# Linear attention and a bilinear feed-forward on one core: inputs of units 4 to 6 loaded later, two weight pieces in their place, and a new order of tiles

## The chip, the cores and the metric

The kernel runs on one core of a Trainium2 chip. The metric is device time in microseconds (us) of that core for one launch. A core has five engines with a queue each: TensorE (PE, matmuls), VectorE (DVE), ScalarE (ACT), GpSimd (POOL) and SyncE (SP), which here only issues DMAs.

## What is computed

A gated linear attention, followed by a feed-forward layer with a product in the middle. All in float32, with `q`, `k`, `v`, `f_logit` of shape (4, 8, 768, 48):

```python
f = 1.0 / (1.0 + np.exp(-f_logit))
for t in range(S):                      # S = 768, per batch and head
    state = f[t][:, None] * state + outer(k[t], v[t])
    y[t] = q[t] @ state
x = y.transpose(0, 2, 1, 3).reshape(B * S, H * D)   # (3072, 384)
out = ((x @ w_a) * (x @ w_b)) @ w_out               # 384 -> 1536 -> 384
```

The weights come in a 64-bit format and have to be turned into float32 on the core before they can be used.

## The kernel before

**Attention** is cut into 16 units. A unit is four heads of one batch over half of the sequence (384 tokens). The two units of a half make a block of 384 tokens: units 0 and 1 block 0, units 2 and 3 block 1, and so on. Each unit's inputs f, k, q and v lie in one of three sets of tiles (`sets[u % 3]`), and `load_unit(u, names)` puts their loads in SP's queue: two DMAs each for f, k and q and one for v. A unit goes through these steps: `front` (ACT: sigmoids; POOL: an affine step; DVE: scans and the scaling of k and q), `scores` (PE) and `mask` (DVE), `turn` (PE transposes k into PSUM) and `turned` (ACT copies it out), `within` (PE: the part of y inside a chunk), `gains` (PE: the growth of the state) and `carried` (DVE sums the states), `across` (PE: the part of y from the states), `out_of_bank` (copies y out of PSUM) and `stored` (DMAs that put it into `xT`, the transposed input of the feed-forward). `y_of(u)` is the last two together. A unit uses two PSUM tiles, `ps_x` and `ps_y`, in turn with its neighbours: `turn(3)` writes the tile from which unit 2's y is copied.

**Weights** come in 20 pieces, called `todo` and counted here from 0: pieces 0 to 13 are columns of `w_b` and `w_a` in turn, 14 to 19 rows of `w_out`. Pieces 0 and 1 hold tile 0 of 128 columns, 2 and 3 tiles 1 and 2, 4 and 5 tiles 3 and 4, 6 and 7 tiles 5 and 6, 8 and 9 tiles 7 and 8, 10 and 11 tiles 9 and 10, 12 and 13 tile 11. `load_weights(n)` issues the next n loads; apart from pieces 4 and 5, they go to four places in turn (`raw`), so the load of piece i waits until the piece that lies in its place has been read. `begin(n)` puts the conversion's first two steps of the pieces below n into the queues: four ACT operations (L58, L59, L62, L63) and one on POOL (L60). `end(n)` adds the rest on DVE (L68, L73, three parts, one for each third of the rows) and, for most pieces, the load of one more piece. `begin(7.5)` stands for a piece's first step alone. `convert(n)` is `end` up to n with the next `begin`.

**Feed-forward up** in this stage is done by tiles: `up(blk, ft)` computes tile ft of both products for block blk, with three matmuls for b and then three for a, into two of four PSUM banks (`ps_f`). `product()` takes the oldest tile not yet multiplied: ACT copies b to `x_sums` (L615) and DVE multiplies a by it into `groups` (L617). After that the two banks are free.

**Order.** All of it stands in `by_quotients` within a manual schedule: each engine executes its instructions in the order in which the program gives them, with semaphores between engines. From the start to unit 3's y the order is written out by hand. Then the loop over `ups` does 14 tiles of blocks 0 and 1, in each round with `convert(needed(i))`, `up`, `end(7 + n)`, `product()` and `begin(ended[0] + 2)`. What follows (the rest of the tiles, units 4 to 15, `down`, and from block 2 on a scheme of products with fewer multiplications) is ordered by a planner that works with assumed durations; it does not use the loading of units 4 to 6.

In the kernel before, `stored(u)` itself loads unit u + 3 for u of 2 and 3, so the inputs of unit 5 stand in SP's queue right behind unit 2's y, and those of unit 6 right behind unit 3's. Unit 4's f is loaded early (at `scores(2)`), its k, q and v after unit 6's inputs.

Of the kernel before, what the change touches and what calls it, by code (L numbers as in the profile page):

```python
# [136 lines left out]
def by_quotients(ctx, tc, q, k, f_logit, v, moe_w_a, moe_w_b, moe_w_out, out, ident, weights, bad):  # L137
# [4 lines left out]
    NKT, NFT, DM = w_ba.shape[2], w_out.shape[1], out.shape[1]  # L142
    NH = S // BLK
    NQ = H // 4
# [6 lines left out]
    NSET = 3  # L151
# [47 lines left out]
    def load_unit(u, names="fkqv"):  # L199
        for do in loads_of(u, names):  # L200
            do()
# [37 lines left out]
    def load_weights(n=1):  # L239
        for _ in range(n):  # L240
            if len(raws) == len(todo):
                return
            dst, src, (k, m) = todo[len(raws)]
            raw = dst
            if src.dtype != FP32:

                if len(raws) in EARLY:
                    raw = groups[:, EARLY.index(len(raws))].bitcast(mybir.dt.uint64)
                else:
                    raw = next(raw_places)  # L250
                raw = raw[:, 0:k * m].rearrange("p (k m) -> p k m", k=k)
            nc.sync.dma_start(out=raw, in_=src)
            raws.append(raw)

    def begin(n):

        while 2 * n > begun[0] < 2 * len(todo):
            i, second = divmod(begun[0], 2)
            dst, src, shape = todo[i]
            if not second:  # L260
                going.append(
                    from_double(
                        nc, dst, raws[i], shape[0], next(blocks), bits[i % len(bits)], sign, whole, shape[0] == NKT
                    )
                    if src.dtype != FP32 else iter(())
                )
            next(going[i], None)
            begun[0] += 1

    def end(n):  # L270

        while ended[0] < min(n, len(todo)):
            begin(ended[0] + 1)
            next(going[ended[0]], None)
            ended[0] += 1
            if ended[0] > 2 and ended[0] - 1 not in EARLY:
                load_weights()
# [15 lines left out]
    def halves(x):  # L293
        return x.rearrange("p n s -> p (n s)")
# [59 lines left out]
    def tokens(n, c, p):  # L354

        return slice(n * BLK + c * C + p * SUB, n * BLK + c * C + p * SUB + SUB)

    def each():
        for n in range(2):
            for c in range(NC):  # L360
                yield n, c, (n * NC + c) * SUB
# [5 lines left out]
    def home(u):  # L367

        return ps_y if u in (1, 3) else ps_x
# [5 lines left out]
    def pair_of(x):  # L375

        return [x[:, i] for i in range(2)]

    def scores(u):
        t = sets[u % NSET]  # L380
        qf, kf = halves(t["q"]), halves(t["k"])
        ps = pair_of(home(u))
        for n, c, o in each():
            for h in range(2):
                for p in range(2):
                    r = slice(R * h, R * h + D)
                    nc.tensor.matmul(  # L387
                        ps[h][SUB * p:SUB * p + SUB, o:o + SUB],
                        lhsT=kf[r, tokens(n, c, p)],
                        rhs=qf[r, tokens(n, c, p)],  # L390
                        start=True,
                        stop=True,
                    )

    def mask(u):

        at = sb1.tile([128, 2, BLK], FP32, tag="at", name="at")
        to, x = (y.rearrange("s h (o t) -> s h o t", t=SUB) for y in (at, home(u)[:, :, 0:BLK]))
        tri = causal.unsqueeze(1).unsqueeze(1)
        nc.vector.tensor_tensor(to, x, tri.broadcast_to((128, 2, 2 * NC, SUB)), ALU.mult)  # L400
        live[u]["at"] = at

    def turn(u):

        kf = halves(sets[u % NSET]["k"])
        live.setdefault(u, {})["kT"] = sb1.tile([128, 2, NC, 128], FP32, tag="kT", name="kT")
        ps = live[u]["turned"] = [ps_f[idle.pop(0)] for _ in range(2)] if u in FIRST else pair_of(away(u))
        for n in range(2):
            for c in range(NC):
                o = n * BLK + c * C  # L410
                nc.tensor.transpose(ps[n][:, c * C:c * C + C], kf[:, o:o + C], ident)  # L411
# [10 lines left out]
    def gains(u, chunks=range(NC)):  # L422

        _, half, _ = unit(u)
        t, kT = sets[u % NSET], live[u]["kT"]
        last = half == NH - 1
        ps = live[u]["turned"]
        for n in range(2):
            for c in chunks:
                for p in range(2):  # L430
                    if last and c == NC - 1 and p == 1:
                        continue
                    for h in range(2):
                        r = slice(SUB * p, SUB * p + SUB)
                        nc.tensor.matmul(  # L435
                            ps[p][R * h:R * h + D, (n * NC + c) * D:(n * NC + c) * D + D],
                            lhsT=kT[r, n, c, R * h:R * h + D],
                            rhs=t["v"][r, n, c, h * D:h * D + D],
                            start=True,
                            stop=True,  # L440
                        )
        if chunks[0]:
            return
        st = sb3.tile([128, NJ, 2, D], FP32, tag="st", name="st")
        before = live[u - NQ]["st"][NJ] if half else None
        live[u]["st"] = [before] + [st[:, j] for j in range(NJ - 1 if last else NJ)]

    def carried(u, js=range(NJ)):

        for j in js:  # L450
            if j + 1 < len(live[u]["st"]):
                carry(u, j)
        if js[-1] == NJ - 1:
            give_back(live[u]["turned"])
# [38 lines left out]
    def across(u):  # L493

        b, half, qd = unit(u)
        qf, st, ps = halves(sets[u % NSET]["q"]), live[u]["st"], live[u]["y"]

        order = [(n, c, o, p) for n, c, o in each() for p in range(2)]
        if u in FIRST:

            order = sorted(order[::-1], key=lambda x: -x[3])
        elif half:
            order = [(n, c, o, p) for n, c, o in reversed(list(each())) for p in range(2)]
        for n, c, o, p in order:
            j = 2 * c + p
            if j == half == 0:
                continue
            for h in range(2):
                r, e = slice(R * h, R * h + D), R * (p ^ h)
                nc.tensor.matmul(  # L510
                    ps[p][e:e + D, o:o + SUB],
                    lhsT=st[j][r, n],
                    rhs=qf[r, tokens(n, c, p)],
                    start=False,
                    stop=True,
                    skip_group_check=True,
                )
# [13 lines left out]
    def stored(u):  # L531

        for do in stores_of(u):
            do()
        if u >= NQ:
            load_unit(u + NSET)

    def stores_of(u):

# [43 lines left out]
    def up(blk, ft):  # L583

        for _, _, _, do, *args in up_steps(blk, ft):
            do(*args)
# [22 lines left out]
    def product():  # L609

        if not factors:
            return
        blk, ft, ps = factors.pop(0)
        b_sb = next(b_copies)
        nc.scalar.copy(b_sb, ps["b"][:, 0:BLK])  # L615
        a, b = (x.rearrange("p (g t) -> p g t", g=NTG) for x in (ps["a"][:, 0:BLK], b_sb))
        nc.vector.tensor_tensor(products(blk)[:, :, ft], a, b, ALU.mult)  # L617
        give_back(ps.values())
# [321 lines left out]
    with tc.manual_schedule():  # L940
# [9 lines left out]
        fronts = {u: front(u) for u in (0, 1, 3)}  # L950
# [95 lines left out]
        product()  # L1046
        carried(2)
        begin(6)
        next(fronts[3])
        up(0, 2)  # L1050
        across(2)
        end(6)
        y_of(2)
        load_weights(2)
        turn(3)
        turned(3)
        scores(3)
        product()
        begin(7)
        up(0, 3)  # L1060
        mask(3)
        begin(7.5)
        within(3)
        gains(3)
        product()
        carried(3)
        begin(8)
        up(0, 4)
        end(8)
        begin(9)  # L1070
        across(3)
        y_of(3)
        load_unit(4, "k")
        load_unit(4, "q")
        load_unit(4, "v")
        product()


        ups = [(0, 5), (1, 0)]
        for i in range(6, NFT):  # L1080
            ups += [(1, i - 5), (0, i)]
        ups += [(1, i) for i in range(NFT - 5, NFT)]
        alone = len(todo) - 6
        for n, (blk, i) in enumerate(ups[0:alone]):
            convert(needed(i))
            up(blk, i)
            end(7 + n)
            product()
            begin(ended[0] + 2)


        w_out_sums, (w_before, w_over) = list(combine_w_out()), combine_w_ba()
# [520 lines left out]
```

## Time and profile before

| what | value |
|---|---|
| median of 3 runs | 606.46 us (605.02 to 607.68) |
| the profiled execution | 607.98 us, its span 606.3 us |
| mean granted PE clock | 0.983 |
| PE busy | 571.5 us, 94% of the span |
| PE weight load busy | 511.3 us, 84% |
| DVE busy | 411.3 us, 68% |
| ACT busy | 268.6 us, 44% |
| POOL busy | 77.2 us, 13% |
| chain that ended last | PE 84%, DVE 8%, DMA 3%, issue 2%, ACT 2% |

The span runs from the first to the last instruction of the core; the device time is somewhat longer. Busy shares are means over the whole span. The chain is followed back from the last instruction, at each step to what released it. In rows of the timeline the columns are start, length, engine, line, operation, tile written and tiles read, count, and in brackets the idle time just before with what ended it. A tile in `up` shows as 12 matmuls[...].

### The profile page before, as it was taken

How to read it: one execution, taken by the hardware profiler on the slowest of the kernel's cores; microseconds unless marked ns; L12 is line 12 of the kernel's file. 1: busy time of each engine (PE TensorE's matmuls, PEld its weight loads, DVE VectorE, ACT ScalarE, POOL GpSimd, SP SyncE). 2: the span in 40 equal slices, each digit the busy share in tenths (PEclk: the TensorE clock that was granted, in tenths of full speed). 3: DMA queues.
4: the chain of work that ended last, by engine and by line, in shares of the span. 5: the costliest groups of instructions: out<-in, count | busy, mean ns of one | idle time of the engine just before them, and what ended most of it. 6: DMA issues, size and time to landing. Idle time of an engine off the chain costs nothing.

```text
span 606.3 us, 13891 instructions
## 1 busy us (share of the span) xinstructions
PE 571.5 (94%) x5778; PEld 511.3 (84%) x5778; DVE 411.3 (68%) x788; ACT 268.6 (44%) x505; POOL 77.2 (13%) x71
## 2 busy tenths in 40 slices
PE   1588799999999999999999999999999999999995
PEld 1555355556899999999989999999999999999995
DVE  6996344579969769967895768746775165745741
ACT  6488658962232455336532353326331335134300
POOL 6344234534200000000000000000000000000000
PEclk9988989999999999999999999999999999999998
DMA  9695796149843143035002420023001100000000
GB/s 208 188 282 160 255 230 206 52 73 172 160 126 105 50 96 79 3 91 133 3 1 78 113 61 2 1 69 77 2 2 47 47 0 1 2 27 0 1 28 32
DMA packets 33272, 49.42 MB, mean 82 GB/s; under 512 B 3952, under 2 KB 24976, under 8 KB 33200
## 3 DMA queue, kind: packets, MB, share of 16 engines
q1 hardware_dynamic: 30000, 42.38, 25.5%
q0 software_dynamic: 3056, 5.92, 5.7%
q8 instruction: 47, 0.77, 0.6%
q14 instruction: 25, 0.20, 0.1%
q10 hardware_dynamic: 144, 0.15, 0.1%
HBM read 33.23 MB, written 4.72 MB: 63 GB/s over the span
## 4 chain that ended last, share of the span: by engine, by line
PE 84%; DVE 8%; DMA 3%; issue 2%; ACT 2%; SPq 1%; DVEq 0%; ACTq 0%
PE ps_f L717 35%; PE ps_f L810 27%; PE ps_f L595 14%; PE ps_y L484 2%; PE ps_x L387 2%; DVE sums L709 1%; PE ps_y L510 1%; DVE inv L329 1%; PE ps_x L411 1%; PE ps_x L435 1%; DMA raw<-in_moe_w_b_dram 1%; DMA xT<-y 1%; DVE groups L709 1%; DVE q_in L333 1%; DVE groups L316 1%
## 5 line engine op out<-in xcount | busy, mean ns | idle before, releaser
L595 PE MATMUL ps_f<-xT,w_ba 128*128 128x384 f32 x288 | 102.2, 513 | 8.0 <-DMA xT<-y 5.7
L595 PEld LDWEIGHTS ps_f<-xT,w_ba 128*128 128x128 f32 x288 | 56.4, 200 | 49.0 <-issue 12.7
L1261 ACT COPY sums<-ps_f 128x384 f32<-128x384 f32 x120 | 57.5, 480 | 75.8 <-PE ps_f L717 68.1
L1261 ACT COPY groups<-ps_f 128x384 f32<-128x384 f32 x120 | 57.8, 481 | 62.8 <-PE ps_f L717 39.9
L717 PE MATMUL ps_f<-xT,w_ba 128*128 128x192 f32 x384 | 78.4, 327 | 0.0
L717 PEld LDWEIGHTS ps_f<-xT,w_ba 128*128 128x128 f32 x384 | 64.8, 190 | 0.2
L717 PE MATMUL ps_f<-groups,w_ba 128*128 128x192 f32 x288 | 55.4, 327 | 0.0
L717 PE MATMUL ps_f<-x_sums,raw 128*128 128x192 f32 x288 | 54.0, 331 | 1.2 <-DVE groups L709 0.9
L810 PE MATMUL ps_f<-w_out,sums 128*128 128x192 f32 x288 | 52.2, 329 | 0.0
L810 PE MATMUL ps_f<-w_out,groups 128*128 128x192 f32 x288 | 51.7, 328 | 0.0
L717 PEld LDWEIGHTS ps_f<-x_sums,raw 128*128 128x128 f32 x288 | 46.9, 190 | 4.3 <-DVE groups L709 1.8
L810 PE MATMUL ps_f<-spare,sums 128*128 128x192 f32 x288 | 49.0, 326 | 0.0
L717 PEld LDWEIGHTS ps_f<-groups,w_ba 128*128 128x128 f32 x288 | 47.9, 190 | 0.5 <-ACT groups L1261 0.3
L810 PEld LDWEIGHTS ps_f<-w_out,sums 128*128 128x128 f32 x288 | 47.1, 190 | 1.0 <-DVE o L845 0.5
L810 PEld LDWEIGHTS ps_f<-w_out,groups 128*128 128x128 f32 x288 | 47.1, 190 | 0.7
L60 POOL TENSOR_SCALAR sums<-sums 128x768 f32<-128x768 f32 (+1 forms) x20 | 40.4, 2021 | 55.6 <-ACT sums L58 55.6
L810 PEld LDWEIGHTS ps_f<-spare,sums 128*128 128x128 f32 x288 | 47.1, 190 | 0.1
L312 POOL TENSOR_SCALAR inv<-inv 128x768 f32<-128x768 f32 x14 | 12.8, 916 | 266.4 <-ACT inv L309 266.3
L709 DVE TENSOR_TENSOR sums<-sums,groups 128x768 f32<-128x768 f32 x36 | 34.7, 965 | 14.2 <-ACT groups L1261 13.7
L709 DVE TENSOR_TENSOR sums<-ps_f,sums 128x384 f32<-128x384 f32 x60 | 32.8, 553 | 16.5 <-PE ps_f L717 15.0
L617 DVE TENSOR_TENSOR groups<-ps_f,x_sums 128x384 f32<-128x384 f32 x24 | 13.2, 553 | 41.2 <-PE ps_f L595 20.4
L717 PE MATMUL ps_f<-x_sums,w_ba 128*128 128x192 f32 x192 | 39.3, 327 | 0.5 <-DVE sums L709 0.5
(135 smaller groups left out, 880.5 us busy)
## 6 DMA issues: line engine op xcount, KB each, us to landing
raw<-w_ba POOLq DMA_DIRECT2D x11, 512.0 KB, 8.0
k_in<-in_k_dram SPq DMA_DIRECT2D x32, 144.0 KB, 3.4
q_in<-in_q_dram SPq DMA_DIRECT2D x32, 144.0 KB, 4.2
v_in<-in_v_dram SPq DMA_DIRECT2D x16, 288.0 KB, 5.0
raw<-in_moe_w_out_dram SPq DMA_DIRECT2D x6, 768.0 KB, 4.2
out_dram<-o SPq DMA_DIRECT2D x24, 192.0 KB, 1.9
f_in<-in_f_logit_dram SPq DMA_DIRECT2D x28, 144.0 KB, 3.0
xT<-y SPq DMA_DIRECT2D x45, 72.0 KB, 2.2
```

What stands on the lines that cost most here:

```text
L60: nc.gpsimd.tensor_scalar(h, h, HI_MAX, None, ALU.min)
L312: nc.gpsimd.tensor_scalar(inv, inv, EXP_K, 1.0, ALU.mult, ALU.add)
L316: nc.vector.tensor_tensor_scan(F[:, c], F[:, c], none, math.exp(MIDDLE), ALU.mult, ALU.add)
L329: nc.vector.tensor_tensor_scan(inv[:, w], inv[:, w], none[:, 0:C], first, ALU.mult, ALU.add)
L387: nc.tensor.matmul(ps[h][SUB * p:SUB * p + SUB, o:o + SUB], lhsT=kf[r, tokens(n, c, p)], rhs=qf[r, tokens(n, c, p)], start=True, stop=True,)
L484: nc.tensor.matmul(ps[p][e:e + D, o:o + SUB], lhsT=t["v"][r, n, c, h * D:h * D + D], rhs=at[r, h, o:o + SUB], start=o == 0, stop=True, ski ...
L595: nc.tensor.matmul(ps[nm][:, 0:BLK], lhsT=w[:, kt, ft * 128:ft * 128 + 128], rhs=xT[blk][:, kt], start=kt == 0, stop=kt == NKT - 1,)
L617: nc.vector.tensor_tensor(products(blk)[:, :, ft], a, b, ALU.mult)
L709: nc.vector.tensor_tensor(to, x, y, op)
L717: nc.tensor.matmul(ps[:, g], lhsT=sums_of_w[name][:, g, 128 * j:128 * j + 128], rhs=sums_of_x[blk][name], start=start and g == 0, stop=Tru ...
L810: nc.tensor.matmul(to, lhsT=x[:, i // 2, i % 2], rhs=w[:, NI * (i % 2) + i // 2], start=start and i == 0, stop=i == HFT - 1, skip_group_ch ...
L1261: do(*args)
```

## The change

Unit 5's and 6's inputs are no longer loaded by `stored`, and unit 4's k, q and v no longer after unit 3's y. They are loaded in rounds n = 3, 5 and 7 of the loop over `ups`, one unit at a time. In SP's queue, the loads of pieces 8 and 9 thereby come right behind unit 2's y, 10 and 11 next, then unit 3's y, 12 and 13, unit 4's k, q, v, two pieces of `w_out`, unit 5, two pieces, unit 6 and the last two pieces.

`end(5)` comes ahead of the last part of unit 3's `front` (the scaling of k and q). `up(0, 3)` moves ahead of `turn(3)`, and `up(0, 4)` ahead of `within(3)`. The product of tile (0, 2) stands ahead of `up(0, 3)`. Between `gains(3)` and `across(3)` no tile is left. The product of tile (0, 4) comes ahead of unit 3's y instead of after it; the conversion of piece 7 comes after the product of (0, 3). The list `ups` starts with (0, 5), (0, 6), (1, 0), (0, 7), (1, 1), ... where it was (0, 5), (1, 0), (1, 1), (0, 6), ... The same tiles are computed; the number of instructions on PE, DVE, ACT and POOL is unchanged. From the third tile of the loop on, the order on PE differs only in which block a tile belongs to.

```diff
         for do in stores_of(u):
             do()
-        if u >= NQ:
-            load_unit(u + NSET)
...
         begin(6)
-        next(fronts[3])
         up(0, 2)
         across(2)
+        end(5)
+        next(fronts[3])
         end(6)
         y_of(2)
         load_weights(2)
+        product()
+        up(0, 3)
         turn(3)
         turned(3)
         scores(3)
+        begin(7)
+        mask(3)
+        up(0, 4)
         product()
-        begin(7)
-        up(0, 3)
-        mask(3)
-        begin(7.5)
+        begin(8)
         within(3)
         gains(3)
+        carried(3)
         product()
-        carried(3)
-        begin(8)
-        up(0, 4)
+        end(7)
+        begin(9)
         end(8)
-        begin(9)
         across(3)
         y_of(3)
-        load_unit(4, "k")
-        load_unit(4, "q")
-        load_unit(4, "v")
-        product()
-        ups = [(0, 5), (1, 0)]
-        for i in range(6, NFT):
-            ups += [(1, i - 5), (0, i)]
-        ups += [(1, i) for i in range(NFT - 5, NFT)]
+        ups = [(0, 5), (0, 6)]
+        for i in range(7, NFT):
+            ups += [(1, i - 7), (0, i)]
+        ups += [(1, i) for i in range(NFT - 7, NFT)]
         alone = len(todo) - 6
         for n, (blk, i) in enumerate(ups[0:alone]):
             convert(needed(i))
...
             product()
             begin(ended[0] + 2)
+            if 2 < n < 2 + 2 * NSET and n % 2:
+                load_unit(NSET + n // 2, "kqv" if n == 3 else "fkqv")
```

## The prediction

> **What bounds the kernel now.** I read the page first, then the chain that ended last, then the timelines of the four engines and SP's queue over 26 to 130 us. Pieces of weights count from 0 (the ninth and tenth are pieces 8 and 9), `up(b,i)` is tile i of block b.
>
> The page says that TensorE (PE) works nearly all the time after the first fifth:
>
> ```profile
> PE   1588799999999999999999999999999999999995
> PEclk9988989999999999999999999999999999999998
> ```
>
> A slice is 15.2 us. The edits lie in slices 3 to 6, where PE has 7 to 9 tenths and the clock is below full. From 81 us the windows show PE busy all the time. So this stage is worth what PE loses in it, and later stages only inherit a shift. PE's waits from 26 to 100 us:
>
> ```profile
> PE ps_f L595 <- DMA xT<-y: 5.7, 3, 4.1
> PE ps_f L595 <- ACT x_sums L615: 2.1, 1, 2.1
> PE ps_x L411 <- ACT y L529: 1.6, 1, 1.6
> ```
>
> Of the first, 4.1 us is at 28 us, ahead of all edits. What is left: 1.61 us before `turn(3)` (50.05), and 2.12 + 0.63 + 1.02 = 3.77 us in `up(1,0)` (69.4 to 75.3). The chain names the cause of the second:
>
> ```profile
> 57.93 0.43 SPq L211
> 58.36 0.04 issue
> 58.40 7.47 DMA raw<-in_moe_w_b_dram
> ...
> 69.51 0.45 ACT y L529
> ```
>
> Piece 8 was issued only at 58.40, behind unit 5's seven loads in SP's queue, and landed at 65.87. ScalarE (ACT) stood at it:
>
> ```profile
> 65.95 0.92 ACT L58 ACTIVATE sums<-raw 128x768 f32<-128x768 f32 x1 [4.68 <-DMA raw<-in_moe_w_b_dram]
> ...
> 69.51 1.43 ACT L529 COPY y<-ps_y 128x384 f32<-128x384 f32 x3
> 70.97 0.86 ACT L615 COPY x_sums<-ps_f 128x384 f32<-128x384 f32 x2
> ```
>
> Unit 3's y and the copies that free PE's banks queue behind. PE's windows (length, busy, matmuls, clock, DMA share, GB/s) show a second cost:
>
> ```profile
> 49.58:52.99 3.41, 1.80 (x77) 1.00 0.13 37
> 52.99:56.41 3.42, 3.42 (x33) 0.50 0.30 76
> ...
> 66.65:70.06 3.41, 2.73 (x9) 1.00 0.89 335
> 70.06:73.47 3.41, 1.33 (x4) 1.00 0.20 57
> 73.47:76.89 3.42, 2.40 (x5) 0.50 0.73 186
> 76.89:80.30 3.41, 3.41 (x7) 0.50 1.05 225
> 80.30:83.71 3.41, 3.41 (x12) 1.00 1.09 212
> ```
>
> After a window with 1.6 or 2.1 us idle the clock is 0.50 until a full window has been busy; 0.7 us idle did nothing. `up(1,0)` and the next tile end just before their products on VectorE (DVE):
>
> ```profile
> 80.67 0.56 DVE L617 TENSOR_TENSOR groups<-ps_f,x_sums 128x384 f32<-128x384 f32 x1 [8.17 <-issue]
> ...
> 84.56 0.56 DVE L617 TENSOR_TENSOR groups<-ps_f,x_sums 128x384 f32<-128x384 f32 x1 [1.73 <-PE ps_f L595]
> ```
>
> So the third tile of the loop over `ups` ends at about 84.5; at 3.87 us a tile from `up(0,5)`'s start at 65.24 it would be 76.9. The loss is 7.6 us, half of it clock.
>
> [...]
>
> **The change, part by part.** To 50.05 us all engines do the same. Durations are those of the profiled execution.
>
> *SP.* Unit 5's seven loads leave the place before pieces 8 to 11. Pieces 8 and 9 are issued at about 55.0 and 55.5, after unit 2's stores, and at the slowest landing seen for such a piece (8.7 us median for w_b) piece 8 is there by 63.7. Unit 6's seven and unit 4's five loads leave the place ahead of pieces 12 and 13. All 19 now go between the `w_out` pieces, five or seven at a time, some 3.3 us of issue each. POOL's queue keeps its order.
>
> *`up(0,3)` ahead of `turn(3)`.* It covers the 1.61 us. But it needs pieces 4 and 5 sooner. DVE: state sums end 48.8; piece 4 (1.60) to 50.4, its thirds from 49.7 on, so the b half starts at 50.05 and ends at 52.0; then unit 3's k and q (1.74) to 52.1, then piece 5, whose first third is there at 53.15. PE waits **1.15 us**; the a half ends at 55.1. `turn(3)` thus starts at 55.1, 3.5 later than before.
>
> *ACT behind it.* Unit 3's k-transpose copy follows (56.0 to 56.7), then piece 6 (3.56) to 60.3, a bank copy (0.36), piece 7 (3.56) to 64.2, the bank copy of (0,4) to 64.7, then piece 8, landed by then, to 68.1; y at 68.1 to 69.5. The 4.68 us wait is gone, but y comes only 1.4 us earlier, as ACT's work stands in a row.
>
> *PE meanwhile.* Scores to 56.5, `up(0,4)` to 60.5, `within` and `gains` to 61.75. DVE's sums of states (1.40) follow `gains`, and no tile stands between as before: PE waits **1.5 us** for `across(3)`, done at 64.05. `up(0,5)` needs piece 6, which DVE takes up only after the product of (0,4) that waits for ACT at 64.7: 0.47 + 0.58 + 0.4 gives 66.15, a wait of **2.1 us**. 3.6 us idle in 4.4 us must halve the clock for about one more busy window: it costs 1.1 to 1.95, I take 1.7 (half of 3.4).
>
> *Sum.* `up(0,5)` ends at 66.15 + 3.9 + 1.75 = 71.8, `up(0,6)` at 75.7: it needs no new piece and no y of block 1. Unit 3's y took 5.8 us from first copy to the last matmul's release, so it lands at 73.9, 1.8 us before `up(1,0)` asks: the 3.77 us stall costs nothing. `up(1,0)` ends at 79.55. Then `up(0,7)` needs piece 9, which DVE takes up after the product of (1,0); its first third is there at 81.05, the a half asks at 81.5: nothing, by 0.45 us. Two pieces in a row on ACT (to 85.0) delay the copy for (0,7); its banks are free at 86.0, asked for at 87.3: nothing.
>
> 84.5 - 79.55 = **4.95 us** gained at the third tile. Later orders on PE, DVE, ACT and POOL are the same and PE is full, so the gain stays.
>
> *Loads put later.* Hidden while the `w_out` pieces land in time. A piece is asked for when its place is free, some 12 us ahead of ACT's need (the first: issued at 85.59, taken up at 98.41); issue of a unit (3.3) and landing (4.2 alone, 8.7 crowded) leave 0 to 4.5 us. Unit 4's k is first needed at about 133, units 5 and 6 later still, all landed by about 100. I take zero; at the other end one late piece is 4 us on PE.
>
> The profiled execution took 607.98 us (span 606.3 and 1.7 around it); less 4.95 is 603.0. The median of the runs shown is 606.46, 1.5 lower, which gives 601.5 if both kernels share that. Part of the 1.5 is probably the unlucky window at 73.5 to 80.3[...], which the change removes anyway; I take **602.0**.
>
> **Rivals.**
> *The first wait also halves the clock.* 1.15 us lies under the 1.6 that did it and over the 0.7 that didn't. Then the a half is slow, `turn(3)` and ACT's row start up to 1.7 later, and so does all behind: gain 3.3, 603.7. [...] Chance 0.17.
> *The stall only moves.* If `up(0,5)` waits longer than worked out (ACT's row takes longer, two slow windows), 3 to 5 us go again: 605 to 607. Against it: the row is made of durations that repeat within 2%. Chance 0.07.
> *Slower: `w_out` pieces come late.* Units 5 and 6 stand ahead of pieces 16 and 18 in SP's queue. When a piece lands more than 12 us after its place is free, ACT stands at it with the bank copies behind, and PE runs out of banks: as before, but up to three times, 3 to 4 us each with the clock, 608 to 612. For it: such a queue made the old stall. Against it: the twelve loads of units 6 and 4 with pieces 12 and 13 (2 MB) went through in about 14 us from 73.6, landing included, and here a unit and a piece (1.5 MB) have 12 to themselves, with no PE wait behind until they are past. Chance 0.08.
>
> **How the numbers follow.** A measurement here can tell about 0.5% (3.0 us) from no change: faster is below 603.4. The forecast has 0.68 and spans 600.5 to 603.4 by the clock's 1.1 to 1.95 and the doubt on the profiled run. Faster: nearly all of it and a third of the first rival, 0.70. Same: 0.20. Slower: 0.10. The range 600.3 to 605.5 leaves out the slower rival, most of the one that moves the stall, and a tail below.
>
> **What would show it.** Right: no wait of ACT for a weight piece at 61 to 66; in PE a gap of about 1.2 inside `up(0,3)`, 1.5 before `across(3)`, 2.1 before `up(0,5)` released by DVE's w_ba (L73), none for xT in `up(1,0)`; the product of the third tile near 79.6. Wrong: a DMA wait on ACT between 85 and 120, a gap in PE after 80, or clock 0.50 in `up(0,3)`.

## The result, and the profile after

The changed kernel took 605.29 us (median of 9 runs, 604.23 to 607.00) against 607.67 us of the kernel before beside it; the ratio is 0.9971, with an interval of 0.9950 to 0.9992. A second set of 22 runs gave 604.76 us and a ratio of 0.9972 (0.9960 to 0.9983). It is faster by about 1.7 us, where 4.5 us were forecast.

In the page of the changed kernel PE is fuller in the second and fourth slice. The clock is higher than before in the fourth and sixth slice (9 tenths for 8), but lower in the third and fifth (7 for 8 and 9):

```profile
PE   1689799999999999999999999999999999999995
PEclk9979799999999999999999999999999999999999
```

PE's waits between 27 and 130 us (total us, times, longest us):

```profile
PE ps_f L593 <- DMA xT<-y: 4.7, 1, 4.7
PE ps_f L593 <- DVE w_ba L73: 2.2, 1, 2.2
PE ps_y L510 <- DVE st L464: 1.5, 2, 1.2
```

The first is the wait at 28 us that both kernels have. The waits ahead of `turn(3)` and in `up(1,0)` are gone. In their place stand those that the prediction named, ahead of `up(0,5)` (2.2 us) and `across(3)` (1.2). PE's timeline shows where:

```profile
51.27 0.89 PE L510 MATMUL ps_x<-q_in,st 48*48 48x64 f32 x48
52.09 4.44 PE L593 MATMUL ps_f<-xT,w_ba 128*128 128x384 f32 x12
...
64.67 1.16 PE L510 MATMUL ps_y<-q_in,st 48*48 48x64 f32 x48 [1.22 <-DVE st L464]
68.00 37.38 PE L593 MATMUL ps_f<-xT,w_ba 128*128 128x384 f32 x107 [2.17 <-DVE w_ba L73]
```

The first line is `across(2)`. It starts at 51.27, not at 49.16 as in the kernel before, although nothing that it waits for was moved. From 68.00 on PE has no gap, to 105 us. ACT no longer waits for a weight piece:

```profile
65.39 0.46 ACT L613 COPY x_sums<-ps_f 128x384 f32<-128x384 f32 x1
65.74 0.89 ACT L58 ACTIVATE sums<-raw 128x768 f32<-128x768 f32 x1
...
69.27 1.43 ACT L529 COPY y<-ps_y 128x384 f32<-128x384 f32 x3
```

PE's windows (length, busy, matmuls, clock, DMA share, GB/s), cut so that the changes of the clock at 66.5 and 73.3 us fall on edges, hold the largest single cost:

```profile
63.16:66.57 3.41, 1.46 (x70) 0.99 0.68 212
66.57:69.98 3.41, 1.98 (x3) 0.50 0.52 196
69.98:73.40 3.42, 3.42 (x7) 0.51 0.19 49
73.40:76.81 3.41, 3.41 (x12) 1.00 0.68 166
```

The half clock (0.50 and 0.51) lasts two windows, of which PE works 5.4 us. At half speed some 2.7 us of these are lost, an estimate from these lines (in a busy window 7 matmuls at 0.51, 12 at 1.00). The third tile of the loop ends just before this line of DVE:

```profile
82.58 0.56 DVE L615 TENSOR_TENSOR groups<-ps_f,x_sums 128x384 f32<-128x384 f32 x1 [1.72 <-ACT sums L58]
```

In all profiled executions of this study, the time less the start of the third tile's product is 523.1 to 523.8 us. So "the third tile" below, the start of that product, stands for the time, and "the stage" for the stretch from the start of `across(2)` to it.

### The profile page after: what moved, and what is told of

Same layout as the page of the kernel before. It is cut to its first block, busy times and chain, and to the rows that moved or that the text cites. A ratio compares the mean times of both kernels' runs of the same rounds, so it can differ in the third digit from the quotient of the medians.

```text
span 604.0 us, 13895 instructions
## 1 busy us (share of the span) xinstructions
PE 571.5 (95%) x5778; PEld 512.5 (85%) x5778; DVE 412.9 (68%) x788; ACT 267.9 (44%) x505; POOL 76.6 (13%) x71
## 4 chain that ended last, share of the span: by engine, by line
PE 87%; DVE 7%; issue 2%; ACT 2%; DMA 1%; SPq 0%; DVEq 0%; ACTq 0%
PE ps_f L715 35%; PE ps_f L808 28%; PE ps_f L593 16%; PE ps_y L484 2%; PE ps_x L387 2%; PE ps_y L510 2%; PE ps_x L411 1%; PE ps_x L435 1%; DVE inv L329 1%; DVE sums L707 1%; DVE groups L707 1%; DVE groups L316 1%; DMA f_in<-in_f_logit_dram 1%; DVE q_in L333 1%; DMA xT<-y 1%
## 5 line engine op out<-in xcount | busy, mean ns | idle before, releaser
L715 PE MATMUL ps_f<-xT,raw 128*128 128x192 f32 x192 | 39.4, 328 | 0.0
```

What stands on the lines that cost most here:

```text
L715: nc.tensor.matmul(ps[:, g], lhsT=sums_of_w[name][:, g, 128 * j:128 * j + 128], rhs=sums_of_x[blk][name], start=start and g == 0, stop=Tru ...
```

## The experiments

Ratios are to the kernel before, timed beside each set.

**Both kernels again.** Unchanged copies, for more profiled executions, in three sets.

> The kernel before, unchanged, for a second profiled execution. Theory A[...]: matmuls of up(0,0) start anywhere from 31.9 to 33.2 us and up(0,1) ends between 43.7 and 46; the two waits (1.6 us ahead of turn(3), some 3.8 us in up(1,0)) recur within 0.5 us, and the third tile of the loop ends between 83.5 and 86. Theory B (the profile of before was an unlucky execution in the stage that the change touches): the stretch at half clock after 73 us is at most 3.4 us, and the third tile ends by 83.

> The changed kernel, unchanged, for a second profiled execution and more times. Theory A: across(2) ends between 50 and 52 us, the waits recur (1.2 us and 2.2 us ahead of across(3) and up(0,5)), the clock is at half for two windows (6.8 us) in most executions, and the third tile ends 30.4 us after across(2) (28.7 where it is one window). Ratio to before 0.995 to 0.998. Theory B: one window, 28.7 us or less, and a ratio of 0.993 or lower in this set.

> The kernel before, for a third profiled execution. The two profiled executions so far took 608.0 and 608.6 us, with a mean clock of 0.983; the middle of the timed runs is 606.4, their clock mostly 0.985 to 0.988. Theory A[...]: an execution near 606.4 has across(2) later than the 49.2 and 49.4 us of those two, or loses one window of clock instead of two after the wait in up(1,0), or none after the wait ahead of turn(3); from across(2) to the third tile it takes 33 to 34 us, not 35.5. Theory D (the changed kernel reaches across(2) later through the change itself): across(2) is at 49.0 to 49.6 again, whatever the time.

> The kernel before once more, for a fourth profiled execution; the same as for the third: Theory A spreads across(2) over 49.2 to 51.3 us, Theory D keeps it at 49.0 to 49.6.

> The changed kernel, for a third profiled execution. Theory A (the start of across(2) is drawn anew in each execution of either kernel, between 49 and 51.6 us, and the prediction set a lucky one against nominal waits): across(2) anywhere in 49 to 51.6 us, from there 30.5 to 31.5 us to the third tile. Theory D (the change itself makes the shared stage slower): across(2) at 50.4 or later.

> The changed kernel, for a fourth profiled execution; as for the third. With four executions of each kernel the means of across(2) can be set side by side: Theory A within 0.7 us of each other, Theory D more than 1 us apart.

| execution | time | across(2) | stage | third tile |
|---|---|---|---|---|
| before, the one shown | 607.98 | 49.16 | 35.40 | 84.56 |
| before_again | 608.61 | 49.39 | 35.73 | 85.12 |
| before_third | 607.35 | 51.00 | 32.73 | 83.73 |
| before_fourth | 607.96 | 50.39 | 34.15 | 84.54 |
| after, the one shown | 605.75 | 51.27 | 31.31 | 82.58 |
| after_again | 604.39 | 50.37 | 30.96 | 81.33 |
| after_third | 605.68 | 50.99 | 31.57 | 82.56 |
| after_fourth | 604.19 | 50.07 | 31.03 | 81.10 |

On the start of `across(2)` Theory A held: it lies anywhere from 49.2 to 51.3 us, in both kernels, and the means (49.99 and 50.68) lie 0.69 apart, just inside the 0.7 allowed. Theory D fell with `before_third` (51.00) and `after_fourth` (50.07). The kernels below share this stretch, except the two that fill the wait at 28 us: with them, six executions with the new order by hand have a mean of 50.7 and nine without it 50.3. The spread arises in `up(0,0)`, which starts at 31.8 to 33.1 us and takes 5.9 to 8.3; from the start of `turn(2)` behind it to `across(2)` it is 11.1 us in all eight.

Theory B fell: the stage of before did not prove an outlier (its mean is 34.50), and the half clock of `before_again` lasted two windows again (73.7 to 80.5 us). The two executions of before that started `across(2)` early had half clock at `up(0,3)` too (53.0 to 56.4 us, and 53.2 to 56.6 in `before_again`) and had the longest stages. Half clock behind the waits of the changed kernel lasted two windows in two executions (66.5 to 73.3 us in the one shown and in `after_third`) and one in the others (68.4 to 71.8 in `after_again`, 68.1 to 71.5 in `after_fourth`). Theory A's sizes for that were a miss: it gave 30.4 us to the stage with two windows and 28.7 with one, and they took 31.3 and 31.6, and 31.0 and 31.0. An execution with one window looks like this (`after_again`):

```profile
65.11:68.52 3.41, 1.24 (x31) 0.99 0.79 232
68.52:71.93 3.41, 3.41 (x7) 0.51 0.10 27
71.93:75.34 3.41, 3.41 (x12) 1.00 0.47 110
```

Here a window ended at 68.52, just after PE was back at work at 67.70; the next was busy throughout at 0.51, and the one behind it had 1.00. In the execution shown first the window from 66.57, at 0.50, still held 1.4 us of idle, and the one behind it had 0.51.

**Loads put later and the new list of tiles, without the new order by hand** (`loads_and_tiles`), as an edit of the kernel before:

```diff
-        if u >= NQ:
-            load_unit(u + NSET)
...
-        load_unit(4, "k")
-        load_unit(4, "q")
-        load_unit(4, "v")
...
-        ups = [(0, 5), (1, 0)]
+        ups = [(0, 5), (0, 6)]
...
+            if 2 < n < 2 + 2 * NSET and n % 2:
+                load_unit(NSET + n // 2, "kqv" if n == 3 else "fkqv")
```

> The loads put later and the new list of tiles, with the order by hand of before. Theory A (what the change loses lies in its new order by hand: turn(3) 3.5 us later sets ACT's row, piece 6 and up(0,5) later, and the clock falls): no wait in up(0,5), up(0,6) or up(1,0), so the clock stays full after 57 us, the third tile ends 27 us after across(2), about 77, 5 us before the changed kernel; ratio 0.986 to 0.991. Rival C (the gain is capped behind the stage, by ACT's conversions of later pieces or by the loads among the w_out pieces): new waits of PE or of ACT for a DMA between 77 and 130 us, and a ratio of 0.994 or above.

It took 600.50 us, ratio 0.9895 (0.987 to 0.992), 4.3 us less than the changed kernel beside it. PE's timeline:

```profile
50.95 0.89 PE L510 MATMUL ps_x<-q_in,st 48*48 48x64 f32 x48
53.45 0.87 PE L411 MATMUL ps_x<-ident,k_in 128*128 128x128 f32 x6 [1.61 <-ACT y L529]
...
65.41 34.77 PE L593 MATMUL ps_f<-xT,w_ba 128*128 128x384 f32 x107
```

Behind the 1.61 us there is no gap any more, the clock is 1.00 from there to 130 us, and the stage takes 26.43 us. Rival C is out: nothing behind the stage takes the gain back. No half clock followed the 1.61 us in this execution, which may be luck. They lie in two windows, 0.35 and 1.26 us:

```profile
48.78:52.19 3.41, 3.06 (x55) 1.00 0.23 56
52.19:55.60 3.41, 2.15 (x56) 1.00 0.19 52
55.60:59.02 3.42, 3.42 (x12) 1.00 0.55 129
```

In `before`, `before_again` and `tiles_only` (below) the same wait lay in one window, and the next was at 0.50: `up(0,3)` then took 5.5 to 5.8 us instead of 4.14. The stage of a single execution can differ by about 1.5 us for this; the timed ratios do not rest on one.

**Each part alone** (`loads_only`, `hand_order_only`, `tiles_only`), with the edits of the change divided as their names say. Each stage but that of all three is from one execution.

> Only the loads put later, with the order by hand and the list of tiles of before. Theory A (the late piece 8 made the wait, the list of tiles hides what is left): ACT takes up piece 8 without a wait, y of unit 3 is copied right after across(3), 15 to 16 us after across(2) started plus 1.4, and lands 1 to 2.5 us after up(1,0) asks for it; one wait of that size for xT is left, and the third tile ends 29 to 31 us after across(2); ratio 0.992 to 0.996. Rival (the list of tiles does the work alone): a wait above 3 us stays and the ratio is 0.998 or above.

> Only the new order by hand, with the loads and the list of tiles of before. Theory A (this part loses): up(0,5) waits 2 us for piece 6, across(3) waits 1.2 us, piece 8 still comes late and up(1,0) still waits for y of unit 3; the third tile ends 35 to 37 us after across(2); ratio 0.999 to 1.004. Rival (the wait ahead of turn(3) was worth its 1.6 us and more): ratio 0.997 or lower.

> Only the new list of tiles, with the loads and the order by hand of before. Theory A (each part alone gains, two of them hide the same wait): ACT still waits 4 to 5 us for piece 8, so up(0,6) waits about 2 us for the banks that the copy behind piece 8 frees, but up(1,0) no longer waits for xT; from across(2) to the third tile 30 to 32 us; ratio 0.993 to 0.998. Rival (without the earlier piece 8 the list moves the wait and nothing more): 34 us or more and a ratio of 0.998 or above.

| parts | ratio | interval | stage |
|---|---|---|---|
| loads | 0.9918 | 0.9894 to 0.9942 | 28.21 |
| list of tiles | 0.9965 | 0.9950 to 0.9981 | 28.41 |
| order by hand | 0.9983 | 0.9970 to 0.9996 | 31.27 |
| loads and list | 0.9895 | 0.9870 to 0.9920 | 26.43 |
| all three | 0.9972 | 0.9960 to 0.9983 | 31.2 (mean) |

With the loads alone, y of unit 3 still lands after `up(1,0)` asks for it:

```profile
65.46 5.49 PE L593 MATMUL ps_f<-xT,w_ba 128*128 128x384 f32 x16
72.42 27.97 PE L593 MATMUL ps_f<-xT,w_ba 128*128 128x384 f32 x86 [1.48 <-DMA xT<-y]
```

That is the wait that the new list hides. Stage and ratio came out a little better than expected. With the list alone ACT still stands at piece 8:

```profile
64.47 0.92 ACT L58 ACTIVATE sums<-raw 128x768 f32<-128x768 f32 x1 [2.63 <-DMA raw<-in_moe_w_b_dram]
```

The wait was 4 to 5 us in the expectation. That execution is the fastest of its 22 (601.75 to 607.27 us), so its stage says little of the others; the 2 us wait for banks that I expected was not in it, and why the times spread so far stays open. The order by hand alone was a miss: I expected a stage of 35 to 37 us and no gain. It took 31.27: ACT reaches piece 8 only at 65.84 there and finds it landed, and `up(0,5)` is so late (68.10) that y of unit 3 is there when `up(1,0)` asks. So in that trace this part alone hides the late piece 8 behind its own waits, and the loads and the list add little once it is in: 0.9983 against 0.9972, with overlapping intervals. Put upon the other two it costs the step from 0.9895 to 0.9972: 4.3 us by the medians of that set, 4.7 by the ratios. The order by hand with only one of the other two was not run, and its single moves were not run apart.

**The new waits filled** (`after_filled`): matmuls that nothing reads.

```diff
+        def filler(n):
+            for _ in range(n):
+                nc.tensor.matmul(
+                    ps_f[idle[0]][:, 0:BLK], lhsT=w_b[:, 0, 0:128], rhs=xT[0][:, 0], start=True, stop=True
+                )
...
         end(8)
+        filler(2)
         across(3)
+        filler(3)
```

> The changed kernel with matmuls that nothing reads put into its two new waits: two of 384 columns ahead of across(3), three ahead of up(0,5), into the bank that up(0,5) starts afresh. They keep PE busy and do no other work. Theory A: the clock no longer falls at 66 us; up(0,5) starts at the same time to 0.3 us and the third tile ends 2.2 to 2.7 us earlier; ratio 0.991 to 0.994. Theory B or C: the clock after the waits is not what is missing: less than 1 us of difference to the changed kernel.

602.99 us, ratio 0.9942 (0.9920 to 0.9965), at the upper end of what Theory A gave. L956 is the filler; each of its five calls shows as two matmuls in the trace:

```profile
63.10 1.56 PE L956 MATMUL ps_f<-xT,w_ba 128*128 128x384 f32 x4
64.59 0.96 PE L510 MATMUL ps_y<-q_in,st 48*48 48x64 f32 x48
65.49 2.20 PE L956 MATMUL ps_f<-xT,w_ba 128*128 128x384 f32 x6
67.67 32.52 PE L593 MATMUL ps_f<-xT,w_ba 128*128 128x384 f32 x100
```

`up(0,5)` starts at the usual time after `across(2)` (16.8 us; 16.7 to 17.4 in the four executions without fillers), but at a clock of 1.00, and the stage is 28.78 us, 2.4 less than the mean of the four. Here useless work in the place of idle made the stage shorter: behind it the clock was 1.00, not 0.50. The stage of all three exceeds 26.43 by 4.8 us. Of these, 2.7 are the later start of `up(0,5)` (17.1 us after `across(2)` in the mean, 14.5 in `loads_and_tiles`), and 2.1 the clock behind it (14.1 us from there to the third tile, 12.0 in `loads_and_tiles` and with the fillers).

**The waits of before filled** (`before_filled`): two such matmuls ahead of `turn(3)`, seven ahead of `up(1,0)`.

> The kernel before with matmuls that nothing reads in its waits: two of 384 columns ahead of turn(3), seven ahead of up(1,0), into PSUM that is started afresh later. Theory A (before's loss in this stage is 5.4 to 6.7 us of waits and 2 to 4 us of clock, drawn anew in each execution): no stretch at half clock after 50 us, from across(2) to the third tile 31 to 32.5 us; 1.5 to 3 us faster than before, ratio 0.995 to 0.9975. Rival (the clock costs before nothing in the middle of its runs, only in slow ones): ratio 0.998 or above, and the lowest of the timed runs no lower than 604.3.

605.91 us, ratio 0.9987 (0.9976 to 0.9997). As Theory A had it, the clock is 1.00 from 50 to 130 us in its profile, and the stage took 31.45 us; but that execution (604.54) is the fastest of its 22, and the timed runs are those of the rival: a ratio above 0.998 and a lowest time above 604.3. In the middle of its runs, the fillers are worth 0.8 us (by the ratio) to the kernel before, little but not nothing.

**Scores ahead of the transposes** (`lt_scores_first`), on top of loads and list:

```diff
+        scores(3)
         turn(3)
         turned(3)
-        scores(3)
```

> Loads put later and the new list of tiles, as in loads_and_tiles, and scores(3) ahead of turn(3): the scores write the other PSUM tile and need k and q, which DVE has ready some 0.5 us after across(2), so they cover part of the 1.6 us in which turn(3) waits for the copies of y. Theory A: the wait is 0.7 to 0.9 us shorter in sum, nothing behind it moves to a later place, the third tile ends 25.5 to 25.9 us after across(2) (26.4 in loads_and_tiles); ratio 0.985 to 0.990. Rival (what stands behind turn(3) on ACT is the limit, as in the changed kernel): 26.4 us or more.

599.21 us, ratio 0.9875 (0.9853 to 0.9897), the best of the study, though its interval overlaps that of loads and list alone.

```profile
51.58 0.89 PE L510 MATMUL ps_x<-q_in,st 48*48 48x64 f32 x48
52.29 0.92 PE L387 MATMUL ps_y<-q_in,k_in 48*64 48x64 f32 x48
54.08 0.87 PE L411 MATMUL ps_x<-ident,k_in 128*128 128x128 f32 x6 [0.87 <-ACT y L529]
```

The wait falls from 1.61 to 0.87 us and the stage to 25.69, as Theory A had it. This covers half of what `up(0,3)` was moved for, and ACT's copy behind `turn(3)` comes no later than without it (3.4 us after `across(2)` in both).

**The wait at 28 us filled** (`lt_early_filled`, `lt_both`): on top of loads and list, and on top of `lt_scores_first`.

```diff
+        for _ in range(14):
+            nc.tensor.matmul(ps_f[2][:, BLK:BLK + 128], lhsT=ident, rhs=ident, start=True, stop=True)
         for u in FIRST:
             stored(u)
```

> As loads_and_tiles, with 14 matmuls of 128 columns that nothing reads in the wait for xT ahead of up(0,0), in the stage that both kernels share. Theory A[...]: no stretch at half clock from 29 to 39 us, up(0,0) takes 4.1 us and not 5.9 to 7.6, across(2) starts at 47 to 48.5; time 597.5 to 599, ratio 0.984 to 0.987. Rival (up(0,0) is held by xT and the DVE conversions, whatever the clock): across(2) at 49 or later and less than 1 us gained on loads_and_tiles.

> The two together: as loads_and_tiles, scores(3) ahead of turn(3) and the 14 matmuls ahead of up(0,0). Theory A: the gains add, across(2) at 47 to 48.5 and the third tile 25.5 to 26 us later; time 596.7 to 598.5, ratio 0.983 to 0.986. Rival (with the earlier stage shorter, the inputs of unit 3 or ACT's conversions become the limit ahead of up(0,3)): a new wait for a DMA or for DVE between 45 and 60 us takes the gain, 599 or more.

Both missed: 601.44 us (0.9916, 0.9891 to 0.9940) and 599.73 us (0.9895, 0.9873 to 0.9916), no faster than without the fillers. In `lt_early_filled` the clock of `up(0,0)` was 1.00, and `across(2)` started at 49.09. But PE then ran ahead of the loads. The chain of that profile:

```profile
36.95 10.66 DMA groups<-in_moe_w_a_dram
...
47.70 0.91 ACT sums L58
```

Piece 5 landed at 47.6, ACT's copies of y of unit 2 queue behind its conversion, `turn(3)` waits 2.6 us instead of 1.6, and the half clock comes there instead (52.7 to 59.5 us). So in that execution, the slowest of its five, the rival was right: a DMA took over as PE got faster. The profile of `lt_both` does not show this. There the clock was 0.50 in `up(0,0)` in spite of the fillers (33.8 to 37.2 us), `across(2)` started at 49.97, and ACT took up piece 5 without a wait; why its median is no lower stays open.

## Why the prediction was wrong

**Right.** The edits act as told. ACT takes up piece 8 without waiting; the 1.61 us and the 3.77 us are gone; `across(3)` waits 1.2 us (1.5 forecast) and `up(0,5)` 2.2 (2.1), in all four executions; `up(1,0)` finds its y; `up(0,7)` has no gap; the loads put later cost nothing, with no wait of ACT for a DMA between 85 and 130 us. With the waits filled, the stage took 28.78 us; the prediction's own stage (79.6 less 49.16, 30.4) without the 1.75 us that it put down to the clock is 28.7.

**Right by luck** is the wait of `up(0,5)`. The gap within `up(0,3)` was 0.3 to 0.7 us instead of 1.15, so ACT was through with the copy of tile (0,4) 14.6 to 15.2 us after `across(2)` started, not 15.5. But the first third of piece 6, put at 0.4 us on DVE, took 0.93 in all four executions. The two errors cancel.

**The step that failed first** is "To 50.05 us all engines do the same. Durations are those of the profiled execution." The order is the same, the time is not: `across(2)` started at 49.16 in that execution, which was the earliest of the eight, and at 50.68 in the mean of the changed kernel's four. The sum set that early start against waits of nominal size. That is 1.5 us of the miss at the third tile. Nor did the early start show in the time of before: where `across(2)` was early its stage was long, and its third tile came at 83.7 to 85.1 in all four. The changed kernel's stage is 31.0 to 31.6 whatever the start.

**The term that was mis-sized** is the stage after the change, 31.2 in the mean instead of 30.4. Half of the 0.8 us is "it costs 1.1 to 1.95, I take 1.7 (half of 3.4)". That is an estimate of the author's: one window at half clock and full clock behind it. In two executions of four the first window at half clock still held 1.4 us of idle, and a second at 0.51 followed. At half speed that makes 2.7 us in these two, 1.7 in the others and 2.2 in the mean, estimates from PE's work at half clock (5.4 and 3.4 us). The lines of before that the prediction shows had the case in them: 73.47 to 76.89 was busy for 2.40 of 3.42 us at 0.50, and the next window was at 0.50 too. Another 0.3 us is the way from the end of a tile to its product: the sum has 11.65 us for three tiles and compares their end with the product of before at 84.5; in `after_filled`, at a clock of 1.00, it is 11.98 from the start of `up(0,5)` to the product. The last 0.1 is the later start of `up(0,5)`.

In sum the third tile came at 81.9 instead of 79.6, 2.6 us before the mean of before's four (84.49), not 4.95. **The rest**: those four took 607.4 to 608.6 us, and the medians of before's timed sets were 606.4 to 607.7, while the changed kernel's four (604.2 to 605.8) lie around its medians. Comparing timed runs, 1.7 us are left. The prediction allowed for 0.5 us of this, as it took 4.95 at the third tile and 4.5 in the median. Why no profiled execution of before was among its faster runs is open.

**Readings that do not hold.** Of before's loss of 7.6 us the prediction put half down to the clock; its windows give 2.9 (an estimate, half of the 5.8 us of work at 0.50). 8.7 us is the median landing of four pieces of w_b, not the slowest seen: `raw` has one of 11.5 in the same trace. That did no harm, as piece 8 landed 4.9 us after its issue, with more than 4 us to spare. From the third tile of the loop on it is the tile and not the block that differs: (1,0), (0,7), (1,1) stand where (1,1), (0,6), (1,2) stood. It cost nothing, as the stretch behind the third tile is of one length in all kernels, to 0.7 us.

**The rivals.** That the first wait halves the clock didn't happen in four executions: `up(0,3)` had its gap of 0.3 to 0.7 us, and the clock was 1.00 behind it. Late `w_out` pieces didn't either. "The stall only moves" was given 0.07 and 605 to 607 us, with its "two slow windows"; it is the closest to what happened, in half of the executions, though `up(0,5)` did not wait longer than worked out.

**What the edits were worth** went in another way than the prediction's account of them suggests: it named the 3.5 us by which `turn(3)` came later (2.6 to 3.3 measured, from `across(2)`), carried it through ACT's row, and counted the result as a gain against before. It did not ask what the other two parts do without it. They give about 6 us; the order by hand takes some 4.5 of these away again.

## What to carry to other kernels

A move that covers a short wait on the busiest engine is costed by what stands behind the moved-past step on the other engines: here 1.6 us were covered, and `up(0,5)`, behind ACT's and DVE's work, began 2.3 to 2.9 us later, with 2.1 us for the half clock on top. Cost the parts of a change one by one and in pairs, not only together: here two parts hid one wait, and a third took most of their gain away. One profiled execution is a draw: here the start of `across(2)` differed by 2.1 us between eight, and the half clock behind the new waits lasted 3.4 us in two of four and 6.8 in the others. Take the start of a stage and its clock from several, or give the range both outcomes.

## What the runs showed of the hardware that was not expected

The same instructions from 0 to 50 us ended 2.1 us apart between the eight executions of the two kernels, with half-clock stretches that began anywhere between 28.9 and 32.4 us. They lasted 6.8 us in seven executions and 10.2 in `after_third`.

The 1.61 us ahead of `turn(3)` were followed by 3.4 us at 0.50 in three executions (`before`, `before_again`, `tiles_only`) and by a clock of 1.00 in four. In the three they lay in one window of 3.41 us, with edges at the changes of the clock in the same trace; in the four they were divided, into 0.35 and 1.26 us in `loads_and_tiles` and into parts of 0.75 to 0.86 us in `before_third`, `before_fourth` and `loads_only`. That is what these seven show, not a rule: in `loads_only` the 1.48 us ahead of `up(1,0)` lay in one window, and the clock behind them was 1.00.

Useless matmuls in 3.4 us of waits made the changed kernel 1.8 us faster (a ratio of 0.9942 for 0.9972); in the kernel before they brought 0.8 us (0.9987), and at 28 us nothing (0.9916 for 0.9895, and 0.9895 for 0.9875).
